# Attention followed by a mixture of experts on one core: each load of q, k or v from the thirteenth on waits for the third load ahead of it

## The chip, the cores and the metric

The kernel runs on one core of a Trainium2 chip. Its metric is the time of one execution on the device, in microseconds (us), the median of several executions. The core has five engines: PE multiplies matrices, DVE (VectorE), ACT (ScalarE) and POOL (GpSimd) compute on vectors, SP computes nothing and issues most of the transfers between the memory and the chip. Transfers are carried out by 16 DMA engines, whichever engine issued them.

## The reference

Eight batches of eight heads of linear attention, each output row normalised by its root mean square, then a mixture of experts on the 4608 resulting rows.

```python
# q, k, v: (8, 8, 576, 64) float32
kv = np.einsum('bhsd,bhse->bhde', k, v)
out = np.einsum('bhsd,bhde->bhse', q, kv)
rms = np.sqrt(np.mean(out * out, axis=-1, keepdims=True) + 1e-06)
x = out / rms * g_norm              # then (B,H,S,D) -> (4608, 512)
do_compute = x @ w_skip > 0         # other rows stay as they are
xc = x[do_compute]
logits = xc @ w_gate                # 8 experts
e_idx = np.argmax(logits, axis=1)   # one expert for each row
for e in range(8):
    m = e_idx == e
    h = np.maximum(xc[m] @ w1[e], 0.0)      # 512 -> 1024
    y[m] = gate_w[m, None] * (h @ w2[e])    # 1024 -> 512
x[do_compute] = xc + y
```

## The kernel before, in words

The program has two stages. In the attention stage (to about 105 us) the core goes through the eight batches. For each batch b it needs k and v (all of both: `state`, L375, sums k transposed times v into the 64 x 64 matrices of the heads) and then q (`turn`, L451, turns pieces of q on PE; `values`, L486, multiplies them with the state). The sums of squares, the roots and the scaling follow on ACT and DVE, the last factor on POOL (`weigh`, L609), and the finished rows of x are stored to the output in memory (`store_x`, L635). While this goes on, rows whose logits are known are given to experts (`gating`, `choose`, `rank`, `number`). In the second stage (from about 110 us) the rows of each expert are gathered from the output in memory, multiplied with its two weight matrices, and scattered back.

The order of the work on each engine is written out by hand: a loop over 40-odd steps (L1013) issues the pieces of one step on all engines, and `at(step, part, job)` puts jobs into a step. Each engine carries out its own instructions strictly in that order, and an instruction that waits holds up all that stand behind it on that engine.

The loads of q, k and v are issued by SP. `load_part` (L115) issues one load: 128 partitions of 576 numbers, 288 KB, a quarter of one of the three inputs of one batch, made of two of its heads. `load_kv` (L128) takes turns between k and v; `load_q` (L137) issues four loads of q. There are 96 loads in all, 12 for each batch. The first 12 are k, v and q of batch 0 (L146 and L147), then k and v of batch 1, q of batch 1, k and v of batch 2. The rest are put into the steps (L979 to L983): k and v of batch b + 3 when the state of batch b is done, q of batch b + 2 two steps after the first step of batch b. The buffers are three deep for k and v and two deep for q (L98 and L99), so a load of a later batch also waits until PE has read what its buffer held.

SP's queue holds the stores of x among the loads: 29 stores of 256 KB, and, behind the last load of q, the loads of the experts' weights (2 MB each, `load_weights`, L334). POOL issues seven further stores of x (L649) and the gathers and scatters of the second stage.

Landings are counted on semaphores, eight for the DMAs of SP and ACT (DMAHW0 to DMAHW7 in the order of the instructions), used in turn. The framework lets a DMA wait until the earlier DMA on its own semaphore has landed.

`tc.add_manual_dep(a, b, WAIT, ...)` adds a wait: instruction a starts only when b is done; if b is a DMA, when it has landed. The kernel uses it in a few other places, for example to hold a weight load until the gathers are out (L340).

Of the kernel before, what the change touches and what calls it, by code (L numbers as in the profile page):

```python
# [17 lines left out]
def kernel(  # L18
# [43 lines left out]
    nc = tc.nc  # L62
# [47 lines left out]
    g_ps = ps_g.tile([P, 512], FP32)  # L110
    GB = 4 * KD + 8 * G

    kts, vts, qts = {}, {}, {}

    def load_part(t, src, b, j):  # L115

        js = slice(j, j + 1)
        nc.sync.dma_start(
            out=t[:, js, :, :].rearrange("p j c d -> p j (c d)"),
            in_=src[b].rearrange("(j a) (p c) d -> (a p) j (c d)", a=2, c=C)[:, js, :])  # L120

    def load(pool, tag, src, b):
        t = pool.tile([P, 4, C, D], FP32, tag=tag, name=tag)
        for j in range(4):
            load_part(t, src, b, j)
        return t

    def load_kv(b, js=range(4)):  # L128
        if b < B:
            if js.start == 0:  # L130
                for name, to in (("k", kts), ("v", vts)):
                    to[b] = kv_pool.tile([P, 4, C, D], FP32, tag=name, name=name)
            for j in js:
                for src, t in ((k, kts[b]), (v, vts[b])):
                    load_part(t, src, b, j)
# [198 lines left out]
    def load_weights(r, pool, behind=None, later=False):  # L334
# [4 lines left out]
        if behind:  # L339
            tc.add_manual_dep(ins.ins, behind.ins.name, WAIT, reason="gathers first")  # L340
        w2 = pool.tile([P, FC, DM], FP32, tag="w2", name="w2")
# [4 lines left out]
    def load_second(r, behind=None):  # L346
# [3 lines left out]
        if behind:  # L350
            tc.add_manual_dep(ins.ins, behind.ins.name, WAIT, reason="gathers first")

# [84 lines left out]

    late = []
    todo = {}
    WAIT = mybir.DependencyInfo(mybir.DependencyClass.Sync, mybir.DependencyReason.SCHED_ONLY)  # L440

    def at(step, part, job):
        todo.setdefault((step, part), []).append(job)
# [180 lines left out]
    def scale(n, behind=None, keep=0, eng=None):  # L624

        while len(late) > keep:
            job, nq, store = late.pop(0)
            ins = job(eng or nc.gpsimd)
            if behind:
                tc.add_manual_dep(ins.ins, behind.ins.name, WAIT, reason="VectorE's port is free then")  # L630
            store = store() if store else None
# [1000 lines left out]
```

## Time and profile before

| | us |
|---|---|
| median of 3 executions | 369.45 (369.28 to 370.48) |
| the profiled execution | 369.93 |
| its span in the profile | 368.1 |
| PE busy in the span | 349.5 (95%) |
| DVE busy | 249.2 (68%) |
| ACT busy | 144.7 (39%) |
| POOL busy | 126.6 (34%) |

The profile is of one execution. Its page gives, among others, the busy time of each engine, the span cut into 40 equal slices with the busy share of each slice in tenths (9 is 90% or more), and the bytes that moved in each. PE is the matrix multiplier itself, PEld its loading of weights, which runs beside it; SPq is SP's sequencer, which issues transfers. A line "A L1 <- B L2: 9.0, 18, 2.0" says that A's instructions of line 1 waited for B's of line 2 for 9.0 us in total, 18 times, at most 2.0 us. The chain of waits follows the work that ended last back from its end, each step to what released it; in it, "issue" is time in which an engine waited for nothing that the profile shows. Times within the execution count from the start of the span.

### The profile page before, as it was taken

How to read it: one execution, taken by the hardware profiler on the slowest of the kernel's cores; microseconds unless marked ns; L12 is line 12 of the kernel's file. 1: busy time of each engine (PE TensorE's matmuls, PEld its weight loads, DVE VectorE, ACT ScalarE, POOL GpSimd, SP SyncE). 2: the span in 40 equal slices, each digit the busy share in tenths (PEclk: the TensorE clock that was granted, in tenths of full speed). 3: DMA queues.
4: the chain of work that ended last, by engine and by line, in shares of the span. 5: the costliest groups of instructions: out<-in, count | busy, mean ns of one | idle time of the engine just before them, and what ended most of it. 6: DMA issues, size and time to landing. Idle time of an engine off the chain costs nothing.

```text
span 368.1 us, 9568 instructions
## 1 busy us (share of the span) xinstructions
PE 349.5 (95%) x3754; PEld 304.4 (83%) x3754; DVE 249.2 (68%) x637; ACT 144.7 (39%) x418; POOL 126.6 (34%) x205
## 2 busy tenths in 40 slices
PE   8979997899889998999999999999999999999994
PEld 4768886788779668599879988988998988989983
DVE  2636677689889661776938675776776876878831
ACT  2537675466666242434204501421431430431420
POOL 8037777667776072223031203303203202002003
PEclk9999999999999999999999999999999999999999
DMA  8999999999977459972617345564663672601001
GB/s 274 383 389 387 393 389 396 401 357 328 325 247 268 116 183 367 363 250 78 230 54 251 98 198 184 176 232 123 223 231 80 241 249 56 244 1 49 11 1 54
DMA packets 32808, 81.70 MB, mean 222 GB/s; under 512 B 3242, under 2 KB 3250, under 8 KB 32756
## 3 DMA queue, kind: packets, MB, share of 16 engines
q1 hardware_dynamic: 28944, 69.48, 53.3%
q0 software_dynamic: 3792, 11.53, 9.3%
q8 instruction: 31, 0.51, 0.5%
q14 instruction: 21, 0.17, 0.1%
q10 hardware_dynamic: 20, 0.02, 0.0%
HBM read 66.80 MB, written 14.48 MB: 221 GB/s over the span
## 4 chain that ended last, share of the span: by engine, by line
PE 78%; issue 8%; DMA 5%; DVE 4%; POOL 3%; ACT 2%; SPq 0%; POOLq 0%; DVEq 0%; ACTq 0%
PE bank L1256 45%; PE bank L1188 8%; PE o_ps L498 6%; DMA v<-in_v_dram 4%; PE sum_ps L383 4%; PE bank L1176 3%; PE q_ps L460 3%; PE bank L1157 2%; DVE xl L545 1%; POOL xb L615 1%; PE g_ps L861 1%; DMA xg<-out_dram,asrc 1%; PE o_ps L508 1%; PE q_ps L861 1%; PE g_ps L762 1%
## 5 line engine op out<-in xcount | busy, mean ns | idle before, releaser
L1266 ACT COPY p<-bank 128x128 f32<-128x128 f32 (+6 forms) x70 | 20.8, 297 | 95.7 <-PE bank L1256 94.1
L1256 PE MATMUL bank<-xt,w 128*128 128x128 f32 (+5 forms) x336 | 55.5, 288 | 0.0
L1387 POOL DMA_INDIRECT out_dram<-xg,rows x14 | 14.0, 997 | 113.4 <-DVE xg L1384 111.1
L1256 PEld LDWEIGHTS bank<-xt,w 128*128 128x128 f32 x336 | 47.0, 190 | 1.9 <-DVE bank L1260 1.4
L615 POOL TENSOR_TENSOR xb<-xl,g_b 128x512 f32<-128x512 f32 x34 | 41.4, 1217 | 19.1 <-DVE rs L536 17.3
L1260 DVE TENSOR_TENSOR bank<-bank,p 128x128 f32<-128x128 f32 (+6 forms) x70 | 23.6, 337 | 29.1 <-PE bank L1256 27.7
L1256 PE MATMUL bank<-xs,s 128*128 128x128 f32 (+5 forms) x224 | 36.7, 288 | 0.0
L498 PE MATMUL o_ps<-kvd,qT 128*128 128x146 f32 x240 | 35.2, 288 | 1.3 <-DVE xl L545 1.0
L498 PEld LDWEIGHTS o_ps<-kvd,qT 128*128 128x128 f32 x240 | 31.4, 189 | 2.1 <-DVE xl L545 1.8
L1256 PEld LDWEIGHTS bank<-xs,s 128*128 128x128 f32 x224 | 31.1, 190 | 1.0 <-issue 0.5
L1188 PE MATMUL bank<-w,ht 128*32 128x128 f32 (+2 forms) x424 | 29.9, 313 | 0.0
L383 PE MATMUL sum_ps<-v,k 64*64 64x64 f32 x1152 | 24.4, 223 | 5.5 <-issue 4.6
L383 PEld LDWEIGHTS sum_ps<-v,k 64*64 64x64 f32 x1152 | 20.0, 134 | 10.0 <-issue 6.9
L545 DVE TENSOR_TENSOR xl<-o_ps,rs 128x584 f32<-128x584 f32 x32 | 24.5, 767 | 4.3 <-PE o_ps L498 0.5
L1188 PEld LDWEIGHTS bank<-w,ht 128*32 128x32 f32 (+2 forms) x424 | 18.2, 119 | 10.6 <-issue 7.2
L1256 PE MATMUL bank<-t,ht 128*128 128x256 f32 x112 | 27.0, 384 | 0.0
L522 DVE TENSOR_REDUCE rs<-sq 128x8 f32<-128x512 f32 x36 | 24.5, 680 | 3.7 <-ACT sq L514 3.6
L1256 PE MATMUL bank<-w,ht 128*128 128x256 f32 x112 | 26.5, 380 | 0.0
L1148 POOL DMA_INDIRECT xg<-out_dram,src x14 | 14.0, 998 | 36.3 <-DMA out_dram<-xg,rows 13.2
L1256 PE MATMUL bank<-t,hs 128*128 128x256 f32 x112 | 25.3, 379 | 0.0
L514 ACT ACTIVATE sq<-o_ps 128x512 f32<-128x512 f32 x34 | 20.3, 597 | 12.5 <-PE o_ps L498 11.8
L463 ACT COPY qT<-q_ps 128x512 f32<-128x512 f32 x32 | 18.8, 586 | 13.5 <-PE q_ps L460 13.3
(216 smaller groups left out, 667.5 us busy)
## 6 DMA issues: line engine op xcount, KB each, us to landing
w<-in_moe_w_dram SPq DMA_DIRECT2D x16, 2048.0 KB, 8.9
k<-in_k_dram SPq DMA_DIRECT2D x32, 288.0 KB, 6.0
v<-in_v_dram SPq DMA_DIRECT2D x32, 288.0 KB, 6.1
q<-in_q_dram SPq DMA_DIRECT2D x32, 288.0 KB, 5.8
out_dram<-xb SPq DMA_DIRECT2D x29, 256.0 KB, 6.4
out_dram<-xb POOLq DMA_DIRECT2D x7, 256.0 KB
xg<-out_dram,src POOLq DMA_INDIRECT x16
out_dram<-xg,rows POOLq DMA_INDIRECT x16
```

What stands on the lines that cost most here:

```text
L383: nc.tensor.matmul(out=sum_ps[w * 64:(w + 1) * 64, a, u, :], lhsT=kt[r, 2 * u + w, c, :], rhs=vt[r, 2 * u + w, c, :], start=(c == 0), stop ...
L463: nc.scalar.copy(out=qT[:, :, :, :].rearrange("p w a t -> p (w a t)"), in_=ps[:, :, :, :, :].rearrange("p w a h t -> p (w a h t)"))
L498: mm = nc.tensor.matmul(out=ps[:, w, 0:2 * PK].rearrange("p (r k) -> p r k", r=2)[:, :, cols], lhsT=qT[:, w, a, :], rhs=kvds[b % KVD][:, w ...
L514: nc.scalar.activation(out=sq[:, :, :, :], in_=heads(ps, G, G + 2 * D), func=ACT.Square)
L522: nc.vector.tensor_reduce(out=rs[:, :, :], in_=sq[:, :, :, :].rearrange("p x y (a d) -> p x (y a) d", a=2), axis=AX.X, op=ALU.add)
L545: nc.vector.tensor_tensor(out=xl[:, :, :, :].rearrange("p x y (a k) -> p x (y a) k", a=2), in0=ps[:, :, 0:2 * PK].rearrange("p x (h k) -> ...
L615: late.append((lambda eng: eng.tensor_tensor(out=xb[:, :, 4 * u * D:(4 * u + 4) * D].rearrange("p r (w x) -> p r w x", w=2), in0=xl[:, :, ...
L1148: nc.gpsimd.indirect_dma_start(out=x_of(xg, off, m), out_offset=None, in_=cut_rows(m)[:, :], in_offset=bass.IndirectOffsetOnAxis(ap=idx[:, ...
L1188: nc.tensor.matmul(out=yps[q * m:(q + 1) * m, 0:n], lhsT=ht(f)[:, off:off + m], rhs=w_sb[r][1][:, f, q * n:(q + 1) * n], start=(f == 0), s ...
L1256: nc.tensor.matmul(out=out, lhsT=lhsT(i), rhs=rhs(i), start=start and i == 0, stop=i == k - 1, skip_group_check=True)
L1260: nc.vector.tensor_tensor(out=to, in0=x, in1=y, op=ALU.add)
L1266: nc.scalar.copy(out=t, in_=x)
```

## The change

From the thirteenth load of q, k or v on, a load also waits until the third load ahead of it has landed. Stores and weight loads are not counted and get no such wait. The line numbers behind it rise by up to five.

```diff
-    kts, vts, qts = {}, {}, {}
+    kts, vts, qts, loads = {}, {}, {}, []
+    PACED, DEPTH = 12, 3
+    WAIT = mybir.DependencyInfo(mybir.DependencyClass.Sync, mybir.DependencyReason.SCHED_ONLY)
 
     def load_part(t, src, b, j):
 
         js = slice(j, j + 1)
-        nc.sync.dma_start(
+        ins = nc.sync.dma_start(
             out=t[:, js, :, :].rearrange("p j c d -> p j (c d)"),
             in_=src[b].rearrange("(j a) (p c) d -> (a p) j (c d)", a=2, c=C)[:, js, :])
+        if len(loads) >= PACED:
+            tc.add_manual_dep(ins.ins, loads[-DEPTH].ins.name, WAIT, reason="a short queue")
+        loads.append(ins)
...
-    WAIT = mybir.DependencyInfo(mybir.DependencyClass.Sync, mybir.DependencyReason.SCHED_ONLY)
```

## The prediction

> **What bounds the kernel now.** I read the page first: its slices, to see what is full and when.
>
> ```profile
> span 368.1 us, 9568 instructions
> ...
> PE   8979997899889998999999999999999999999994
> ...
> DVE  2636677689889661776938675776776876878831
> ...
> DMA  8999999999977459972617345564663672601001
> GB/s 274 383 389 387 393 389 396 401 357 328 325 247 268 116 183 367 363 250 78 230 54 251 98 198 184 176 232 123 223 231 80 241 249 56 244 1 49 11 1 54
> ```
>
> A slice is 9.2 us. From the second to the eighth the DMA engines are full, at 383 to 401 GB/s, until 74 us; that is most of the attention stage, in which q, k and v come in. Afterwards DMA has room and PE is the bound. So the change, which touches only the loads, acts in the first 90 us. Next the DMA issues (count, KB each, median us from issue to landing) and the waits of SP's queue, which issues all of these loads (us in total, times, longest):
>
> ```profile
> k<-in_k_dram SPq DMA_DIRECT2D x32, 288.0 KB, 6.0
> v<-in_v_dram SPq DMA_DIRECT2D x32, 288.0 KB, 6.1
> q<-in_q_dram SPq DMA_DIRECT2D x32, 288.0 KB, 5.8
> ```
>
> ```profile
> SPq L118 <- DMA v<-in_v_dram: 9.0, 18, 2.0
> ...
> SPq L118 <- DMA q<-in_q_dram: 7.6, 17, 0.9
> SPq L118 <- DMA k<-in_k_dram: 6.4, 17, 0.7
> ...
> SPq L118 <- PE o_ps L498: 2.1, 3, 0.8
> ```
>
> A load lands 6 us after its issue, and SP waits 23 us for landings but hardly for PE. So SP's loads already wait for one another; the order of the instructions will show how. The timeline of SP shows the pace (start, length, instruction):
>
> ```profile
> 14.21 4.13 SPq L118 DMA_DIRECT2D q<-in_q_dram  x4
> 18.76 0.33 SPq L118 DMA_DIRECT2D k<-in_k_dram  x1
> 19.51 0.33 SPq L118 DMA_DIRECT2D v<-in_v_dram  x1
> 20.26 0.33 SPq L118 DMA_DIRECT2D k<-in_k_dram  x1
> 21.03 0.33 SPq L118 DMA_DIRECT2D v<-in_v_dram  x1
> ...
> 45.31 0.37 SPq L118 DMA_DIRECT2D k<-in_k_dram  x1
> ...
> 60.33 0.33 SPq L118 DMA_DIRECT2D k<-in_k_dram  x1
> ...
> 73.09 0.33 SPq L118 DMA_DIRECT2D k<-in_k_dram  x1
> ```
>
> One load is issued every 0.75 us, when one lands: 0.75 us is a load's share of full engines (288 KB at 390 GB/s), and 8 in flight times 0.75 is the 6 us. Last the chain of waits, for how closely PE follows:
>
> ```profile
> 9.97 8.02 DMA v<-in_v_dram
> 17.99 0.34 issue
> 18.33 1.26 PE sum_ps L383 x68
> ...
> 22.03 2.42 issue
> ...
> 45.92 0.59 PE q_ps L460 x4
> ...
> 62.33 0.49 PE q_ps L460 x4
> ...
> 63.71 1.42 issue
> ...
> 70.78 0.74 issue
> ...
> 75.06 0.59 PE q_ps L460 x4
> ...
> 86.80 0.50 PE q_ps L460 x4
> ```
>
> PE waits for a load at 18 us. The four rows of L460 are the turns of q for batches 3, 4, 5 and 6. Before each, q must have landed. The second q load of batch 3 carries the flag on which the issue at 45.31 waits, that of batch 4 the one at 60.33, of batch 5 the one at 73.09. So q lands 0.6, 2.0 and 2.0 us before PE needs it. PE follows the loads at under 2 us: whatever the load stream loses beyond that, PE loses.
>
> **The change part by part.** SP's queue, first at the thirteenth load (k_267 is k of batch 1). Before, eight flags DMAHW0 to 7 go round, and a DMA waits for the earlier user of its own flag, the eighth DMA ahead:
>
> ```order
> L118 DMA k_267<-in_k_dram 128x576 [waits DMAHW0_49]
> L118 DMA v_268<-in_v_dram 128x576 [waits DMAHW1_49]
> L118 DMA k_267<-in_k_dram 128x576 [waits DMAHW2_49]
> L118 DMA v_268<-in_v_dram 128x576 [waits DMAHW3_49]
> L118 DMA k_267<-in_k_dram 128x576 [waits DMAHW4_49]
> L118 DMA v_268<-in_v_dram 128x576 [waits DMAHW5_49]
> ```
>
> The same place after:
>
> ```order
> L120 DMA k_267<-in_k_dram 128x576 [waits DMAHW5_49,DMAHW0_49]
> L120 DMA v_268<-in_v_dram 128x576 [waits DMAHW6_49,DMAHW1_49]
> L120 DMA k_267<-in_k_dram 128x576 [waits DMAHW7_49,DMAHW2_49]
> L120 DMA v_268<-in_v_dram 128x576 [waits DMAHW3_49,DMAHW0_49]
> L120 DMA k_267<-in_k_dram 128x576 [waits DMAHW4_49,DMAHW1_49]
> L120 DMA v_268<-in_v_dram 128x576 [waits DMAHW2_49]
> ```
>
> Nothing moves; the waits now name the third load ahead, so at most three loads (0.86 MB) are in flight instead of eight. The second place is SP's first store of x (xb_483) and the q loads of batch 3 (q_758); before:
>
> ```order
> L653 DMA out_0_dram<-xb_483 64x1024 [waits DMAHW4_49,Pool_49]
> L653 DMA out_0_dram<-xb_483 64x1024 [waits DMAHW5_49]
> L118 DMA q_758<-in_q_dram 128x576 [waits DMAHW6_49,PE_49]
> L118 DMA q_758<-in_q_dram 128x576 [waits DMAHW7_49]
> L118 DMA q_758<-in_q_dram 128x576 [waits DMAHW0_49]
> ```
>
> and after:
>
> ```order
> L657 DMA out_0_dram<-xb_483 64x1024 [waits Pool_49]
> L657 DMA out_0_dram<-xb_483 64x1024
> L120 DMA q_758<-in_q_dram 128x576 [waits DMAHW1_49,PE_49]
> L120 DMA q_758<-in_q_dram 128x576 [waits DMAHW2_49]
> L120 DMA q_758<-in_q_dram 128x576 [waits DMAHW3_49]
> ```
>
> Stores lose their wait for a landing and don't count as loads. Behind each waiting load stand the later loads and the stores of the same queue; for the loads wait PE's state (L383) and q turns (L460), for the stores nobody until the gathers.
>
> The edit's cost is one number: the pace P of loads when each is issued at the landing of the third ahead. One round, from issue to landing, then takes at least 3P. If the round is shorter than 3 x 0.75 = 2.25 us, the engines stay full and P stays 0.75. The trace of before never has so few in flight, so I bound it by transfers that had the engines nearly for themselves: the second load of the program, and four 256 KB stores between 118 and 125 us, where nothing else moves (x count, KB each, median us to landing).
>
> ```profile
> 1.20 3.35 DMA v<-in_v_dram
> ```
>
> ```profile
> out_dram<-xb SPq DMA_DIRECT2D x4, 256.0 KB, 3.0
> ```
>
> The load's 3.35 us hold some 0.3 us behind the first load, issued 0.46 us before it (0.75 - 0.46): 3.05, and the stores say 3.0. So P lies between 0.75 and 3.05 / 3 = 1.02. It is nearer to the upper row, since even a small transfer needed 3.0; but with two loads still moving ahead some of the start-up is hidden. I take a round of 2.75 us, P = 0.92.
>
> The Trainium skill ("DMA: Bandwidth & Descriptors", Anatomy of one DMA) fits one DMA as 2.0 us plus bytes over 436 GB/s, for the GpSimd path: an estimate of 2.68 us here, P = 0.89, and the sum below would be about 1 us smaller. The rows above read 3.0, so the fixed part looks larger here than the fit's.
>
> The sum, stage by stage, along the loads that PE follows. From the landing of the thirteenth load (14.21, its flag releases the first q of the x4) to the second q load of batch 3 (45.31) come 37 loads in 31.1 us: 37 x 0.75 = 27.75, and 3.35 us for two SP stores, a POOL store and other traffic. After: 37 x 0.92 = 34.0; of the 3.35 us I let half fall into the gaps that the slower pace leaves, 1.7 stay: 35.7, so 4.6 us later. The 0.6 us of room are used first: PE's turn at 45.92 comes 4.0 us later.
> To batch 4 there are 16 loads in 15.0 us (12 + 3.0): after, 14.7 + 1.5 = 16.2, and PE itself takes 62.33 - 45.92 = 16.4: nothing is added. To batch 5, 12 loads in 12.8 us (9 + 3.8): after, 11.0 + 1.9 = 12.9 against PE's 12.7: nothing to speak of. To batch 6, PE takes 11.7, and 12 loads with the same share some 11.0 + 1.3 = 12.3: with the 0.1 of room left, 0.5 more. Sum 4.5 us. What follows (the last turns, the routing, the experts) hangs on PE and DVE and starts that much later; the expert weights are issued behind these loads by data that DVE makes, and move along.
>
> Is the loss swallowed later? DVE would have to be the bound already. In windows of 10 us (PE, PEld, DVE, ACT, POOL busy):
>
> ```profile
> 60.00:70.00 10.00, 7.62 (x163) 6.86 (x163) 6.24 (x17) 5.08 (x14) 6.06 (x11) 1.00 1.05 400
> ...
> 90.00:100.00 10.00, 8.85 (x137) 7.86 (x136) 8.85 (x27) 6.64 (x20) 6.84 (x13) 1.00 0.98 329
> ```
>
> DVE has room at 60 us, none to speak of at 90. I count nothing back. The removed waits of the stores cost and gain nothing: nobody waits for a store there. The extra flag on some loads is a wait on a landing that is already past: nothing.
>
> The bounds: with P = 1.02 and a third of the other traffic left, 37.7 + 1.1 gives +7.7, less 0.6; then 16.3 + 1.0 against 16.4 adds 0.9, 12.2 + 1.3 against 12.7 adds 0.8, 12.2 + 0.8 against 11.7 adds 1.3: about +10. With P = 0.80: 29.6 + 2.7 = 32.3, +1.2, less 0.6 of room: +0.6, and 0 at 0.78.
>
> The profiled execution took 369.93 us (span 368.14), 0.48 above the median of 369.45. A shift of 4.5 makes 374.4 of the one and **374.0** of the other.
>
> **The rivals.** *Full engines and shorter pauses: faster.* PE's three pauses with "issue" at 22.03, 63.71 and 70.78 (2.42, 1.42 and 0.74 us) lie in the middle of L383, whose loads have landed. PE's instructions come by the same DMA engines:
>
> ```profile
> q8 instruction: 31, 0.51, 0.5%
> ```
>
> ```profile
> PE 349.5 (95%) x3754; PEld 304.4 (83%) x3754; DVE 249.2 (68%) x637; ACT 144.7 (39%) x418; POOL 126.6 (34%) x205
> ```
>
> 31 packets of 16.5 KB for about 7,500 instructions, 68 bytes each: a block every 242 instructions, and L383 is where PE issues fastest. If a block waits behind eight loads, three loads would let it come sooner. This decides if P stays under about 0.78. But PE can't run ahead of its q: the gain stops at the room before batch 4 and 5, 2.0 us, or 367.5. The Trainium skill ("Runtime: NRT & Kernel Launch", Instruction fetch mechanics) has these 16 KiB blocks, and calls their cost mostly hidden; the 31 packets agree on the size, and by "hidden" this rival would gain nothing. Chance 0.11.
> *The round just fits: no change.* P of 0.78 to 0.81, the cost (up to 1) met by shorter pauses: 369.5. For it speaks that other traffic keeps the engines warm; against it both rows near 3.0. Chance 0.12.
> *Fully exposed: much slower.* P = 1.02: 379.5. For it, both rows; against it, two loads still moving ahead. Chance 0.15.
> *Swallowed by DVE:* the 4.5 shrink to some 2.5, 372, if DVE's work up to 100 us is the true bound of this stage. The 6.24 speaks against it. Chance 0.12.
>
> **How the numbers follow.** The forecast itself has 0.50. A measurement of this kernel can tell about 0.3%, 1.1 us, from no change. Faster by more has 0.11, within it 0.12, slower 0.77 (0.50 + 0.15 + 0.12). The range from 369.0 to 379.8 leaves out the first rival and what lies past the third, under 2 in 10; the forecast's own range, P from 0.85 to 0.98, is 371.3 to 378.
>
> **What the profile after would show.** Right: loads land some 2.8 us after issue instead of 6, SP waits on landings for longer, issues are 0.9 us apart, GB/s in slices 2 to 5 falls to about 340 (390 x 31.1 / 35.7), and PE shows waits for q at L460 or for k and v at L383 of some 4 us between 30 and 50 us, none of note after 62. Wrong: issues 0.75 us apart and GB/s at 390 with three in flight (P hidden); the "issue" pauses gone and the later stages earlier by as much; or DMA waits as forecast with the start of the experts unmoved.

## The result, and the profile after

| | before | after |
|---|---|---|
| median, us | 369.62 (369.28 to 370.48, 6 executions) | 407.05 (403.22 to 410.38, 6 executions) |
| the profiled execution, us | 369.93 | 403.22 |
| its span, us | 368.1 | 401.4 |

The changed kernel is slower: ratio 1.098, 95% interval 1.0941 to 1.1018. That is 37 us where 4.5 were forecast, and far outside the range. The table gives medians of all six executions; the ratio compares the means, without the slow one of after (410.38). The profiled execution is the fastest of the six, and 33.3 us longer in its span than that of before, so the traces below show 33 of the 37 us. The direction was right, the size wrong by a factor of eight.

The page after, first the slices (now 10.0 us each):

```profile
span 401.4 us, 9574 instructions
...
PE   8965959685959899989999999999999999999994
...
PEclk9999898968779999999999999999999999999998
DMA  8868888888888994597733545366365545610101
GB/s 268 281 210 277 274 279 279 268 280 264 255 280 248 380 312 111 166 374 299 239 119 151 183 157 211 106 213 224 109 211 210 157 164 209 213 56 0 55 1 50
...
k<-in_k_dram SPq DMA_DIRECT2D x32, 288.0 KB, 4.0
v<-in_v_dram SPq DMA_DIRECT2D x32, 288.0 KB, 3.8
q<-in_q_dram SPq DMA_DIRECT2D x32, 288.0 KB, 3.6
```

Where before moved some 390 GB/s, after moves 210 to 281, and the loads go on into the thirteenth slice, past 120 us, instead of to 74. PE's digits, hardly under 8 before, drop to 5 and 6 in six slices of that time. A load lands 3.6 to 4.0 us after its issue: sooner than the 6 of before, but three in flight at some 3.75 us each are 1.25 us per load. The forecast was 2.75 us, 0.92 and 340 GB/s. The granted clock (PEclk) falls as well, where PE idles; an experiment below asks if that matters.

The waits of SP and PE after (us in total, times, longest):

```profile
SPq L120 <- DMA q<-in_q_dram: 28.5, 24, 4.6
SPq L120 <- DMA k<-in_k_dram: 21.0, 25, 2.5
SPq L120 <- DMA v<-in_v_dram: 16.5, 20, 2.1
...
SPq L120 <- PE q_ps L464: 1.4, 3, 0.6
...
PE q_ps L464 <- DMA q<-in_q_dram: 18.4, 10, 4.8
...
PE sum_ps L388 <- DMA v<-in_v_dram: 7.5, 6, 2.3
```

SP waits 66 us for landings instead of 23, and hardly for PE (the longest such row is the one of 1.4 us): PE itself hardly holds the loads back. (It can through POOL and the stores of x that stand among the loads; the last experiment is about that.) PE waits ten times for q, not once for 4 us as forecast. The chain of waits after:

```profile
13.14 3.33 DMA v<-in_v_dram
16.49 3.29 DMA k<-in_k_dram
19.80 3.85 DMA v<-in_v_dram
23.66 5.32 DMA q<-in_q_dram
29.00 2.79 DMA v<-in_v_dram
31.80 3.00 DMA k<-in_k_dram
34.82 4.76 DMA v<-in_v_dram
39.60 2.83 DMA k<-in_k_dram
42.45 2.99 DMA q<-in_q_dram
...
61.56 0.69 PE q_ps L464 x2
...
82.45 0.69 PE q_ps L464 x2
...
98.94 1.32 PE q_ps L464 x4
...
117.45 1.34 PE q_ps L464 x4
```

Each row of a DMA is one round, issue to landing, and the next one starts when it ends: this is the new wait itself, nine times in a row. The rounds take 2.8 to 5.3 us. The four turns of q that stood at 45.92, 62.33, 75.06 and 86.80 now stand 15.6, 20.1, 23.9 and 30.6 us later; the span ends 33.3 later. So the loss is made while loads come in, in every batch, and what follows keeps it. Two rows of windows (PE, PEld, DVE, ACT, POOL busy, then granted clock, DMA share, GB/s):

```profile
20.00:30.00 10.00, 6.20 (x106) 5.18 (x105) 3.78 (x8) 4.09 (x12) 4.26 (x8) 1.00 0.69 210
...
110.00:120.00 10.00, 5.70 (x69) 5.07 (x70) 4.55 (x16) 2.89 (x10) 3.54 (x9) 0.76 0.88 281
```

PE stands idle for some 4 of 10 us, and DVE is busy for less than half. The DMA engines are counted busy for 0.69 and 0.88 of the time, yet move only 0.54 and 0.72 of the 390 GB/s of before.

### The profile page after: what moved, and what is told of

Its sections match the earlier page's. It is cut to its first block, busy times and chain, and to the rows that moved or that the text cites. A ratio compares the mean times of both kernels' runs of the same rounds, so it can differ in the third digit from the quotient of the medians.

```text
span 401.4 us, 9574 instructions
## 1 busy us (share of the span) xinstructions
PE 362.3 (90%) x3754; PEld 314.2 (78%) x3754; DVE 249.5 (62%) x637; ACT 144.3 (36%) x418; POOL 125.7 (31%) x205
## 4 chain that ended last, share of the span: by engine, by line
PE 68%; DMA 17%; issue 6%; POOL 3%; DVE 3%; SPq 1%; ACT 1%; POOLq 0%; DVEq 0%; ACTq 0%
PE bank L1260 41%; PE bank L1192 9%; DMA q<-in_q_dram 8%; DMA v<-in_v_dram 5%; PE o_ps L502 4%; PE bank L1180 4%; PE q_ps L464 3%; DMA k<-in_k_dram 2%; PE sum_ps L388 2%; PE bank L1161 2%; POOL xb L619 1%; DMA xg<-out_dram,src 1%; SPq L120 1%; PE g_ps L865 1%; PE q_ps L865 1%
## 5 line engine op out<-in xcount | busy, mean ns | idle before, releaser
L1264 DVE TENSOR_TENSOR bank<-bank,p 128x128 f32<-128x128 f32 (+6 forms) x70 | 23.6, 336 | 30.6 <-PE bank L1260 29.3
L464 PE MATMUL q_ps<-ident,q 128*128 128x128 f32 x128 | 25.5, 319 | 18.5 <-DMA q<-in_q_dram 18.4
L502 PE MATMUL o_ps<-kvd,qT 128*128 128x146 f32 x240 | 39.9, 314 | 1.3 <-DVE xl L549 1.0
L502 PEld LDWEIGHTS o_ps<-kvd,qT 128*128 128x128 f32 x240 | 36.3, 214 | 2.3 <-DVE xl L549 1.6
L464 PEld LDWEIGHTS q_ps<-ident,q 128*128 128x128 f32 x128 | 15.6, 159 | 22.8 <-issue 13.6
L388 PE MATMUL sum_ps<-v,k 64*64 64x64 f32 x1152 | 26.1, 231 | 7.5 <-DMA v<-in_v_dram 7.5
L540 DVE RECIPROCAL rs<-rs 128x8 f32<-128x8 f32 x36 | 7.1, 198 | 40.2 <-ACT rs L533 40.2
L1260 PEld LDWEIGHTS bank<-xs,s 128*128 128x128 f32 x224 | 31.1, 190 | 1.0 <-issue 0.5
L388 PEld LDWEIGHTS sum_ps<-v,k 64*64 64x64 f32 x1152 | 21.8, 142 | 12.3 <-issue 7.6
```

Source lines behind the costliest of these rows:

```text
L388: nc.tensor.matmul(out=sum_ps[w * 64:(w + 1) * 64, a, u, :], lhsT=kt[r, 2 * u + w, c, :], rhs=vt[r, 2 * u + w, c, :], start=(c == 0), stop ...
L464: nc.tensor.transpose(out=ps[:, w, :, hf, :], in_=qts[b][:, 2 * u + w, c:c + 2, :], identity=ident[:, :])
L502: mm = nc.tensor.matmul(out=ps[:, w, 0:2 * PK].rearrange("p (r k) -> p r k", r=2)[:, :, cols], lhsT=qT[:, w, a, :], rhs=kvds[b % KVD][:, w ...
L1260: nc.tensor.matmul(out=out, lhsT=lhsT(i), rhs=rhs(i), start=start and i == 0, stop=i == k - 1, skip_group_check=True)
L1264: nc.vector.tensor_tensor(out=to, in0=x, in1=y, op=ALU.add)
```

## The theories and the experiments

Three theories stood against each other at first; the fourth was put together after the first four runs (the loads alone, the same with work on PE, four and five in flight). *Small bare round* (A in the expectations): three loads alone would make about the forecast's round, and stores and instruction blocks make the rest. *Fixed round* (B): a load takes some 3.7 us from issue to landing here, however many are in flight; the pace is 3.7 divided by their number. *Clock* (C): PE waits, its clock is taken down, and the slower PE is a large part of the loss. *Dry engines* (D): a load has landed when the last of 16 engines is done with it; the others run out of work meanwhile and lose time when they start again, the more so the fewer loads are queued; and what holds up one engine (an instruction block, a store) holds up the next issue.

**The loads alone.** Only the 96 loads, five times, with 8, 5, 4, 3 and 2 in flight (names `deep` to `two`); nothing is computed and the output is zeros.

```diff
+        elif depth < 8 and count[0] >= depth:
+            tc.add_manual_dep(ins.ins, loads[-depth].ins.name, WAIT, reason="a short queue")
+    for name, depth in (("deep", 8), ("five", 5), ("four", 4), ("three", 3), ("two", 2)):
```

> This kernel computes nothing: it issues the 96 loads of q, k and v five times over, with up to 8, 5, 4, 3 and 2 of them in flight, each part after the one before has landed, and at the end writes zeros to the output. Two theories of why three in flight made a load cost 1.25 us (37 loads in 46.4 us) and not 0.92. Theory A, the slowest engine: the bare round is near 2.8 to 3.0 us, as forecast, and the rest came from other traffic (stores, blocks of PE's instructions), which delays one of the 16 DMA engines and so the landing. A expects here, with no other traffic: 0.75 us a load with 8, 5 and 4 in flight, 0.93 to 1.0 with 3, 1.4 to 1.5 with 2. Theory B, the bare round: the round is simply longer than forecast, 3.7 us. B expects 0.75 with 8 and 5, 0.93 with 4, 1.25 with 3, 1.85 with 2.

The issues of k in each part (KB, median us to landing), then a window inside each part (DVE, POOL, granted clock, DMA share, GB/s):

```profile
deep<-in_k_dram SPq DMA_DIRECT2D x32, 288.0 KB, 6.0
...
five<-in_k_dram SPq DMA_DIRECT2D x32, 288.0 KB, 4.5
...
four<-in_k_dram SPq DMA_DIRECT2D x32, 288.0 KB, 3.9
...
three<-in_k_dram SPq DMA_DIRECT2D x32, 288.0 KB, 3.3
...
two<-in_k_dram SPq DMA_DIRECT2D x32, 288.0 KB, 3.1
```

```profile
20.00:70.00 50.00, 0.00 (x0) 0.00 (x0) 1.00 1.06 392
90.00:150.00 60.00, 0.00 (x0) 0.00 (x0) 1.00 0.97 330
180.00:245.00 65.00, 0.00 (x0) 0.00 (x0) 1.00 0.93 303
275.00:355.00 80.00, 0.00 (x0) 0.00 (x0) 1.00 0.87 265
385.00:500.00 115.00, 0.00 (x0) 0.00 (x0) 1.00 0.72 189
```

288 KB at these rates are 0.75, 0.89, 0.97, 1.11 and 1.56 us per load. With three in flight and no other traffic at all, a load already costs 1.11: more than the 1.02 that the prediction took for the worst. So the small bare round falls. The round is not fixed either: it goes from 3.1 to 4.5 us with two to five in flight. Both theories had put five in flight at 0.75 us per load, and both were wrong there. The second view shows two losses. The share of busy time falls (1.06 to 0.87 with three): the engines are empty for part of the time. And a busy engine moves less: 392 / 1.06 = 370 GB/s per unit of share with eight, 265 / 0.87 = 305 with three, 262 with two.

The times of the single packets in the traces show where the second loss sits. A load is 128 packets of 2,304 bytes. Most take 94 to 98 ns however many loads are in flight; those over 180 ns take some 400 ns, and their share grows as the queue gets shorter (alone: within the windows above and, for six and seven, those of the parts further below; in the kernel: from 15 us to about the end of the loads, where 8 is the kernel before):

| in flight | 8 | 7 | 6 | 5 | 4 | 3 | 2 |
|---|---|---|---|---|---|---|---|
| loads alone, packets over 180 ns | 0.0% | 0.1% | 0.5% | 3.8% | 5.5% | 8.1% | 12.9% |
| in the kernel | 0.6% | 0.8% | 3.0% | 4.4% | 6.4% | 7.6% | |

With two in flight there are 16.6 long packets per load, about one for each of the 16 engines. That is what an engine would show that runs dry and pays a start-up when its next load comes. That the long packet is the first one after a dry spell is not shown, since the kept traces don't say which engine a packet was on; nor do they say what happens inside it.

The Trainium skill ("DMA: Bandwidth & Descriptors", Why a DMA increments its semaphore by 16 and not by 1) has each of the engines that a DMA uses post its own share of the landing; so the wait ends with the slowest of them, which is what such a loss needs.

**The same with work on PE.** 6,000 small matmuls beside the loads, for the fetches of their instructions; nothing else is computed.

```diff
-    PE_WORK = 0
+    PE_WORK = 6000
```

> The same loads, beside which PE issues 6,000 small matrix products that use none of them, some 12,000 instructions, so that blocks of 256 instructions are fetched all the time; nothing else is computed. Theory A expects 8 in flight to stay at 0.75 to 0.78 us a load, and 3 in flight to rise above the kernel without PE by 0.1 to 0.3 us a load, with rounds of 4 to 5 us where a block passes and 3 elsewhere. Theory B expects the same paces as without PE within 0.05 us.

PE, PEld, DVE and POOL, granted clock, DMA share and GB/s in windows inside the first three parts:

```profile
20.00:70.00 50.00, 31.33 (x1140) 30.59 (x1137) 0.00 (x0) 0.00 (x0) 0.64 1.05 385
90.00:150.00 60.00, 45.07 (x1664) 44.07 (x1664) 0.00 (x0) 0.00 (x0) 0.73 0.96 319
180.00:220.00 40.00, 31.46 (x1187) 30.81 (x1184) 0.00 (x0) 0.00 (x0) 0.83 0.87 270
```

The matmuls ended at 233 us, ahead of the part with three (from 275 us), which therefore tells nothing new; a later experiment has it. With eight in flight the fetches take 2% of the rate (385 against 392), with four 11% (270 against 303). The windows also show that the first rival had a true core: PE gets through 22.8 matmuls per us with eight loads in flight, 27.7 with five, 29.7 with four. It is busy for the same 27 ns per matmul in all three; what differs is its pauses, waits marked "issue": eight of them, 18.5 us in all, in the first window, and eight of 8.5 us in all in the third, so 2.3 us each with eight in flight and 1.1 us with four. Instructions do come sooner behind a short queue.

**The depth in the kernel.** One number of the changed kernel:

```diff
-    PACED, DEPTH = 12, 3
+    PACED, DEPTH = 12, 4          # likewise 5, 6 and 7
```

> The changed kernel with the fourth load ahead in place of the third. Theory A: rounds of 3.2 us and more where an instruction block or a store passes, so 0.85 to 0.95 us a load while the stream of before needs 0.84 with its other traffic; 372 to 382 us. Theory B: 3.7 / 4 = 0.93 us a load, and other traffic on top of it; 380 to 388 us. Theory C, that PE's lower clock after its waits makes most of the loss: the clock goes up with fewer waits, and the loss falls to under a quarter, under 378 us.

> The changed kernel with the fifth load ahead. Theory A: the round may take 3.75 us before it costs anything, so only the rounds with an instruction block cost; 369 to 373 us. Theory B: 3.7 us just fits; 369 to 372 us. If a shorter queue also shortens PE's pauses for instructions (2.4, 1.4 and 0.7 us before), up to 2 us less than the kernel before, 367.5.

> The changed kernel with the sixth load ahead. The loads alone took 0.75 us each with 8 in flight, 0.88 with 5, 0.98 with 4, 1.11 with 3, and 4 and 5 in flight made the kernel 21 and 13 us slower. Theory D, dry engines: each landing waits for the slowest of 16 engines, the others run dry meanwhile, and an engine that has run dry pays a start-up; the fewer loads in flight, the more. D expects some 0.80 us a load with 6, and 373 to 377 us. Theory A, in which 3.75 us of queue should have been enough, expects no loss, 368 to 370 us.

> Each load from the thirteenth on waits for the seventh load ahead instead of the third. Dry engines: with seven in flight the loads alone kept the full pace (0.755 us each), as they did with six, and yet the kernel with six was 1.9% slower, so what the blocks of instructions and the stores delay is not made up. One more load in flight covers most of such a delay (about 0.75 us): 1 to 3 us slower than before, ratio 1.003 to 1.008. If only the bare pace counted, six would have cost nothing and seven costs nothing: ratio 0.997 to 1.003. If shorter pauses of PE were worth anything, this is where they would show, with the engines full: up to 2 us faster, ratio 0.995.

| in flight | us | ratio to before (interval) |
|---|---|---|
| 3 (the change) | 407.05 | 1.098 (1.0941 to 1.1018) |
| 4 | 390.48 | 1.0577 (1.053 to 1.0623) |
| 5 | 381.90 | 1.0339 (1.0284 to 1.0394) |
| 6 | 373.22 | 1.0193 (1.0165 to 1.0221) |
| 7 | 369.34 | 1.0031 (0.9999 to 1.0064) |

The runs are from different chips; each ratio is to the kernel before on the same chip. The cost falls with each further load in flight, from 9.8% to 0.3%, which is not clear of no change, and nowhere turns into a gain. With four and five the kernel was slower than any theory had put it (388 and 373 us at most). Six lies in the range of the dry engines. Seven (1.0031) stands at the border between both its ranges and decides nothing. Six in flight is the row to look at, since six alone keep the engines full (next experiment but one). The kernel's slices with six:

```profile
GB/s 266 370 321 327 388 371 324 375 365 355 364 331 307 118 117 341 394 298 129 228 44 260 78 215 170 185 234 95 247 231 48 273 234 47 263 1 46 14 1 54
```

321 to 388 GB/s: the pace is full in some slices, and lost in others. I take these to be the ones with blocks and stores; with six that was not measured apart. The long packets fit it: 3.0% in this kernel, 0.5% with six loads alone.

**The wait only from the 49th load.** The first 48 loads as before.

```diff
-    PACED, DEPTH = 12, 3
+    PACED, DEPTH = 48, 3
```

> The changed kernel with the wait from the forty-ninth load on instead of the thirteenth. If the loss is a price for each paced load (theories A and D), the second half pays what it paid in the changed kernel, 63.7 us for loads 50 to 96 against 46.4 before, 17.3 us, less the 2 us of room that PE had: 382 to 386 us. If the loss came mostly from the first batches, where PE follows the loads most closely, or from PE's lower clock after long waits (theory C), less than half of the 37 us stays: under 380 us.

387.62 us, ratio 1.0571 (1.0538 to 1.0604): 20.9 us, more than expected, for 48 of the 84 loads (57% of the loads, 56% of the loss). That fits a price for each paced load; the clock theory's figure, under 380 us, is missed. The prediction had put 4.0 of its 4.5 us before batch 4 and nearly nothing behind it.

**Parts of the traffic, and other sizes.** Loads alone again, nothing computed: three in flight beside 3,000 matmuls; three with a 256 KB store behind each third load; three of double size (576 KB); six; seven.

```diff
+    part("three", 3)
+    part("mixed", 3, store=3)
+    part("pair", 3, pair=True)
+    part("six", 6)
+    part("seven", 7)
```

> Loads alone again, in five parts: three in flight while PE issues 3,000 small products (some 24 instruction blocks); three in flight with a store of 256 KB after each third load, not counted; three in flight of double size (576 KB, 48 of them); 6 and 7 in flight. Nothing is computed from the loads, and the output is zeros. Theory A (other traffic makes the round) expects the first part at 1.25 us a load or more and the second at 1.3 or more. Theory D expects the first within 0.1 of the 1.11 without PE, the second near 1.11 + 0.1 (the store fits into time in which engines are dry, but adds to some rounds), the double loads at 1.5 to 1.6 us, which is 0.75 to 0.8 for each 288 KB, since 1.7 MB in flight keep the engines fed, and 0.80 to 0.82 with 6, 0.75 to 0.77 with 7.

Windows inside the five parts (PE, PEld, DVE, POOL, clock, DMA share, GB/s):

```profile
10.00:110.00 100.00, 75.65 (x2852) 73.78 (x2848) 0.00 (x0) 0.00 (x0) 0.87 0.77 229
130.00:245.00 115.00, 0.00 (x0) 0.00 (x0) 0.00 (x0) 0.00 (x0) 0.50 0.90 285
260.00:335.00 75.00, 0.00 (x0) 0.00 (x0) 0.00 (x0) 0.00 (x0) 0.50 0.94 319
350.00:410.00 60.00, 0.00 (x0) 0.00 (x0) 0.00 (x0) 0.00 (x0) 0.50 1.04 389
425.00:485.00 60.00, 0.00 (x0) 0.00 (x0) 0.00 (x0) 0.00 (x0) 0.50 1.05 393
```

Three with the instruction blocks move 229 GB/s, 1.29 us per load, where three alone moved 265. Six and seven keep the full 390. The double loads speak against bytes in flight as the measure: three of 576 KB are as many bytes as six of 288, and move 319 instead of 389. So the number of transfers in line matters, not the bytes alone. The part with stores took 129.3 us (123.6 to 252.9) for its 96 loads, 1.35 each against 1.11 alone: some 0.7 us for each of its 32 stores.

The dry-engines theory had most of these numbers wrong: it put the first part at 1.21 or less (1.29), the second near 1.21 (1.35), the double loads at 1.5 to 1.6 us (89.9 / 48 = 1.87) and six in flight at 0.80 to 0.82 (0.76 in the window). It took other traffic to be too cheap and six to be too slow. The small bare round, wrong about three loads alone, had the first two right: 1.25 or more and 1.3 or more. What holds is a part of each: a longer bare round, whose engines run dry, and other traffic on top of it.

**A warmer PE.** Four extra matmuls of ones ahead of each turn of q from the third step on (work added, for the clock alone).

```diff
+        if n > 1:
+            dense(4, ps[:, :, :, :, :].rearrange("p w a h t -> p (w a h t)"))
```

> The changed kernel with four more matrix products of ones (512 columns, their result overwritten) ahead of each turn of q from the third step on, so that PE works instead of waiting for q. Theory C, that PE's lower clock after its waits (0.66 to 0.91 in windows from 80 to 130 us) makes a good part of the loss: the clock stays at 1 and the time falls by 6 us or more, under 401 us. Theory D, that PE only waits for the loads: the time changes by at most 2 us either way from 407, since a faster PE waits longer.

404.33 us, ratio 1.1063 (1.1016 to 1.1111), where the change alone has 1.098. The clock did not stay at 1, as the experiment meant it to: its mean in the profiled execution rose from 0.962 to 0.979, and the time at half clock until the loads end fell from 27.3 to 13.7 us. Nothing was gained by that half. The extra products can hide a small gain, since they hold up a turn whose q has landed for up to 1.5 us (four of 0.38 us). But a clock that made a large part of 37 us would show here, and SP's loads hardly wait for PE in any case. So the clock theory falls as the main cause; a share of a few us is not ruled out.

The Trainium skill ("TensorE: Matmul & The Clock Gate", Part 1) halves the clock after an idle window of some 3.4 us. The trace of the changed kernel agrees in part: its clock is 0.5 for 3.4 or 6.8 us at a time, at waits of PE of 3.8 to 4.8 us, but also at shorter ones, of 2.3 us (from 40.1 us on) and 2.8 us (from 81.1 us on).

**The parts on one chip.** Loads alone, nothing computed, on one chip within one program, so that bare rounds and disturbed ones can be set side by side: bare (three in flight), blocks (with 3,000 matmuls), stores (a 256 KB store behind each ninth load), both, and deep (eight, the same stores).

```diff
+    part("bare", 3)
+    work()                        # 3,000 matmuls; they start when "bare" has landed
+    part("blocks", 3)
+    part("stores", 3, store=9)
+    work()
+    part("both", 3, store=9)
+    part("deep", 8, store=9)
```

> The 96 loads alone, nothing is computed, in five parts on one chip: bare (three in flight), blocks (the same, with 3,000 small matmuls on PE for their instructions), stores (three in flight, a 256 KB store behind each ninth load, about as in the kernel), both, and deep (eight in flight, the same stores). Dry engines, with what the other parts gave: bare 1.11 us per load, blocks 1.29 (about 0.8 us for each of 22 blocks of 16 KB), stores 1.19 (0.74 us for each of 11 stores), both 1.37: the delays add up, none falls into the gaps; deep 0.83. The prediction's view, that half of the other traffic falls into the gaps: blocks and stores together add half as much, both at 1.24 or less. If the chip and not the blocks made the difference between the two kernels of loads, bare is 1.29 already.

The tiles of k in each part (shortest, median, longest ns of the issue, then first and last start in us), and the queue of the instructions:

```profile
L33 SPq DMA_DIRECT2D bare<-in_k_dram x32: 327/328/432, 0.7 to 98.1; - x32
```

```profile
L33 SPq DMA_DIRECT2D blocks<-in_k_dram x32: 327/328/1132, 106.8 to 220.9; - x32
```

```profile
L33 SPq DMA_DIRECT2D stores<-in_k_dram x32: 327/328/585, 229.6 to 335.2; - x32
```

```profile
L33 SPq DMA_DIRECT2D both<-in_k_dram x32: 327/328/1982, 344.9 to 463.1; - x32
```

```profile
L33 SPq DMA_DIRECT2D deep<-in_k_dram x32: 327/328/502, 472.8 to 544.7; - x32
```

```profile
q8 instruction: 46, 0.75, 0.6%
```

A part starts when the one before has landed, so first start to first start is a part's whole time: bare 106.1 us, blocks 122.8, stores 115.3, both 127.9, or 1.11, 1.28, 1.20 and 1.33 per load. Bare is 1.11 as in the first experiment, and blocks 1.28 where another chip had 1.29, so it isn't the chip that made the difference. 23 of the 46 blocks fall into "blocks": 16.7 / 23 = 0.73 us each. Ten stores: 0.92 each (some 0.7 in the parts above), more than the 0.67 that their bytes take on full engines. "deep", whose last load lands at 554.2 us, took 81.4 us, 0.85 per load: 0.6 us for each store with eight in flight, where loads alone took 75.6. Both together cost 21.8 of the 25.9 that the two cost apart: 84% adds up, where the prediction had let half vanish in the gaps.

How a block makes a load late can be read from the trace. A block is one packet of 16,384 bytes, so it sits on one engine, for 0.9 to 1.8 us here. Each load posts 16 landings, and the wait ends with the last: it comes 0.43 us after the middle of the 16 in "bare", on average over the part, and 0.89 us in "blocks".

**The stores on another queue.** Behind SP's stores of x stand loads of q; where POOL is late with x, the store waits, and q with it, which makes PE and then POOL later. 21 stores moved to POOL, in the changed kernel and in the kernel before:

```diff
-        first = int(i == 1 and b < B - 1)
-        if first:
-            nc.gpsimd.dma_start(out=rows[0], in_=x[0:64, :])
+        first = 2 if b < B - 1 else 0
+        for hf in range(first):
+            nc.gpsimd.dma_start(out=rows[hf], in_=x[hf * 64:(hf + 1) * 64, :])
+        if first:
+            return None
```

> The changed kernel with the 21 stores of x of the first seven batches that SP issues moved to POOL, which issues them right behind the work that makes their rows (0.58 to 0.9 us of POOL each). Behind a store in SP's queue stood the loads of q, and SP's pairs of stores before the q loads of later batches took 1.2, 1.9, 2.1 and 2.0 us, partly in waits for POOL. If this ring (PE late, POOL late, store late, q late) feeds the loss, its removal gives back 3 to 5 us: ratio to the kernel before 1.085 to 1.09. Dry engines alone: the same bytes take the same DMA engines, and the time is that of the changed kernel within 1%: 1.09 to 1.105, or a little more, since POOL has the issues.

> The same move of the 21 stores in the kernel before, without any wait for a landing of the third load ahead: what the move costs or gains by itself. SP waited there for POOL about 8 us in front of stores over the whole stage, with eight loads in flight to cover it; so no gain is expected, ratio 0.995 to 1.01, the upper part because POOL spends some 0.6 to 0.9 us more on each of 21 issues and its last factor comes later.

405.81 us, ratio 1.1059 (1.1019 to 1.1099), and without the short queue 373.19, 1.0161 (1.0129 to 1.0194): no gain in either. The first misses the 1.085 to 1.09 of the ring. The second, 1.6% above the kernel before with an interval that leaves out 1, is slower than I expected. If the move costs the same in both kernels, the short queue costs 1.1059 / 1.0161 = 1.088 with it, instead of 1.098. By that the ring feeds the loss with about 3.5 of the 37 us (1 to 6 with the intervals of the three ratios); it is not the cause.

## Why the prediction was wrong

*What bounds the kernel:* right. PE followed the loads at under 2 us, and what the loads lost, PE lost: at batch 3 the landing comes 16.2 us later and PE's turn 15.6, the 0.6 us of room being used first.

*The change on the queue:* right. The wait does what the order shows. SP's timeline after has the issue that waits for the thirteenth load, and the one that waits for the second q of batch 3:

```profile
15.13 0.33 SPq L120 DMA_DIRECT2D v<-in_v_dram  x1
...
61.53 0.33 SPq L120 DMA_DIRECT2D k<-in_k_dram  x1
```

37 loads in 46.4 us, 1.25 each, where before took 31.1 and the forecast was 35.7.

*"A round of 2.75 us, P = 0.92": this step failed first.* The bounds came from a single transfer with the engines to itself (3.05 and 3.0 us), and I took 3.05 / 3 as the upper end, since "with two loads still moving ahead some of the start-up is hidden". The runs show the reverse: with two in flight a round takes 3.1, with three 3.3, with four 3.9. The start-up isn't hidden: the engines are empty for part of the time, and 8.1% of the packets are long ones. P is 1.10 to 1.11 with nothing else on the engines. The single transfer was a lower bound of the round, not an upper one.

*"Half fall into the gaps": this step failed as much.* In the four stretches to batch 6 the prediction had 1.7 + 1.5 + 1.9 + 1.3 = 6.4 us for stores, blocks and other traffic. Priced by the parts on one chip, with the counts of the trace (blocks on the instruction queue, stores of SP and POOL):

| to batch | loads x 1.10 | (blocks x 0.73 + stores x 0.92) x 0.84 | sum | measured | forecast | before |
|---|---|---|---|---|---|---|
| 3 | 37: 40.7 | 5, 4: 6.2 | 46.9 | 46.4 | 35.7 | 31.1 |
| 4 | 16: 17.6 | 2, 5: 5.1 | 22.7 | 20.9 | 16.2 | 16.4 |
| 5 | 12: 13.2 | 2, 5: 5.1 | 18.3 | 16.5 | 12.9 | 12.7 |
| 6 | 12: 13.2 | 2, 5: 5.1 | 18.3 | 18.5 | 12.3 | 11.7 |
| all | 84.7 | 21.5 | 106.2 | 102.3 | 77.1 | 71.9 |

(Measured and before: 37 loads as above in the first row, turn to turn of the chain in the others; forecast: its times of the loads.) The sum of prices that were measured without the kernel comes within 4% of the kernel over all four stretches, and within 11% in each; with 0.7 for a store it is about 103 in all. Of the 25 us that the forecast lacks, 77 x (1.10 - 0.92) = 14 are the pace, and the rest is other traffic: 84.7 from the measured 102.3 leaves 17.6, against 6.4. The slower pace leaves gaps, but the other traffic doesn't go into them for free: a block makes one engine late, and the load that waits for that engine's landing is issued later by about as much (0.73 us per block).

*"PE itself takes 16.4: nothing is added"*, and the like for batches 5 and 6: wrong, as a consequence. PE's own 16.4, 12.7 and 11.7 us would have covered 16.2, 12.9 and 12.3; they don't cover 20.9, 16.5 and 18.5. Here 15.0 of the 30.6 us arise, and the experiment from the 49th load on shows it in the kernel. The last 2.7 us arise behind batch 6's turn at 117.45 us. The granted clock is 0.50 until 122.0 us there and 1.00 after; that the 2.7 us come from it is not shown, since the warmer kernel gained nothing.

*What follows moves along:* right, the later stage is shifted as a whole and swallows nothing. *DVE* was no bound: it is busy for 3.8 and 4.6 of 10 us in the two rows above.

*The rivals.* Full engines and shorter pauses: the pauses do shorten with a short queue (2.3 to 1.1 us each), and in the kernel "issue" at L383, 4.6 us before, is gone from PE's list of waits, which has waits for loads in its place; but they were worth nothing to a PE that waits for loads. With seven in flight, where the loads alone keep full pace, the kernel gained nothing either (1.0031). The round just fits: it does so alone at six, not at three. Fully exposed, P = 1.02: nearest, and still short by 28 us.

*What stays open:* what an engine does in the long packets, and why six in flight nearly do away with them and five don't. With six the kernel still loses 1.9%, and the long packets are back (3.0% against 0.5% alone): that blocks and stores bring them is argued, not shown. The profiled execution after is the fastest of the six, so 4 of the 37 us stand in no trace.

## What to carry to other kernels

A transfer's time with the engines to itself is a lower bound of its time in a short queue, not an upper one: measure the stream itself, with as many in flight as are meant. A wait for the landing of a load a few places ahead passes the lateness of the slowest engine to the next issue, so price other traffic at nearly its full time on that stream (84% of it here), in every batch. Where a consumer follows the loads closely, keep at least as many loads queued as fill the engines alone, and one or two more for what disturbs them (here six fill them alone, and the kernel needs seven).

## What the runs showed of the hardware

- Loads of 288 KB from one queue need six in flight for full pace: 389 to 393 GB/s with six to eight, 330 with five, 303 with four, 265 with three, 189 with two. Three of 576 KB make 319.
- The 2,304-byte packets of these loads take 94 to 98 ns, but for some of about 400 ns: none with eight in flight, 0.5% with six, 3.8% with five, 8.1% with three, 12.9% with two.
- A 16 KB block of instructions is one packet, 0.9 to 1.8 us on one engine. It costs a stream with three loads in flight 0.73 us, one with eight about 2% of its rate (385 against 392 GB/s, at a block every 5.7 us: 22.8 matmuls and as many weight loads per us, and 46 blocks for 12,000 such instructions).
- Blocks arrive sooner behind a short queue: PE paused 1.1 us for one with four loads in flight, 2.3 us with eight, and did 30% more matmuls per us.
- A 256 KB store costs a stream with three loads in flight 0.7 to 0.9 us, one with eight 0.6 us.
- Moving 21 stores from SP's to POOL's queue cost the kernel before 1.6% by itself; where that comes from wasn't followed.
